# Rows 3 and 4 of a fused attention and squared-ReLU kernel: another order for their loads, copies and transposes

## The chip, the cores and the metric

The kernel runs on one core of a Trainium2 chip. The metric is the device time of one execution in microseconds (us). A core has five engines with an instruction queue each: TensorE (PE in the profile, its weight loads PEld), VectorE (DVE), ScalarE (ACT), GpSimd (POOL) and SyncE (SP), which here only issues DMAs. Every queue is worked off in order: an instruction that waits holds up all that stand behind it on its engine. DMAs are issued from the queues of SP and POOL and carried out by the core's 16 DMA engines.

## The reference

Eight batch rows (`q`, `k`, `v` of 8 heads, 576 positions, 64 dims) go through masked attention. Heads 0 to 3 see a sliding window of 32 positions, heads 4 to 7 see every fourth of the last 128. The result, as 4608 tokens by 512, goes through two matrix products with a squared ReLU between them.

```python
rel = pos[:, None] - pos[None, :]
mask_plain = (rel >= 0) & (rel < 32)
mask_dil = (rel >= 0) & (rel < 128) & (rel % 4 == 0)
scores = where(mask, q @ k.T / sqrt(64), -1e9)
attn = softmax(scores)              # plain mask for heads 0-3, dilated for heads 4-7
x = (attn @ v).transpose(0, 2, 1, 3).reshape(4608, 512)
out = relu(x @ w_in) ** 2 @ w_out   # w_in 512 x 2048, w_out 2048 x 512
```

## The kernel before

The order of all work is written out by hand. Two streams run side by side on TensorE. One is the matrix products, in nine chunks `c` of 512 tokens: first `mm1_gen` (line 263, 16 tiles of 128 features; ScalarE applies the ReLU at line 272 and VectorE squares at line 297), then, for chunks 1 and 2, `mm2_gen` (line 304), and from chunk 3 on `seven_gen` (line 407), which computes the second product with seven instead of eight block products. The other stream is the attention of the rows `b`, eight of them, cut into parts: `z0 z1` (dilated scores, line 613), `s0 s1` (sliding scores, line 599), `d0 d1 e0 e1` (probabilities times `v`, dilated, line 668), `a0 a1 a2` (the same, sliding, line 652), and `y0 y1 x0 x1` (transposes of the result, lines 701 and 683, copied into `xT` by ScalarE at 707 and 689). The products are a Python generator that `pump` advances; `run` pumps to a step number and then issues the part that stands at that step. Chunk `c` carries the attention of row `c+1`; from chunk 2 on it also carries the scores of row `c+2`. So chunk 1 works on row 2, chunk 2 on row 3 and on row 4's scores.

Before the scores of a row can be computed, its `q` and `k` pass through several hands. For the loop's rows this is so:

1. POOL looks (`see`, line 190) at something that has landed, to hold its queue until then, and issues four DMAs: `n` (sliding heads, line 146) and `dd` (dilated heads, line 223, from DRAM to DRAM), `k` and `q` of each, converted to fp16 on the way.
2. `in_token_order` (lines 228 to 236) copies `n` to `o` in token order. For row 2 ScalarE copies 6 of 9 parts and VectorE 3; for every other row VectorE copies all. The step is `ORDER[c]`, so the copy stands in VectorE's queue among that chunk's other work.
3. SP writes `o` to DRAM (`dp`, line 241) and reads both back through the DMA's transpose: `QKTd` from `dd` (line 253), `QKTp` from `dp` (line 249).

The `v` of a row is loaded as fp32 by SP, dilated heads into `sd` (lines 164 and 166, two DMAs) and sliding heads into `sv` (line 156, six DMAs); there is one buffer of each. POOL casts them to fp16: `vd<-sd` in four casts (line 208), `vp<-sv` in three (line 204). `vd` is read by `d0` to `e1`, `vp` by `a0` to `a2`.

At the start of chunk 1 POOL's queue holds: four casts of `sd` (row 2), a look at the last piece of `sv`, a look at row 2's `QKTp`, the four DMAs for row 3, three casts of `sv`. At the start of each later chunk it holds a look at the newest row's `QKTp`, the four DMAs of row `c+2`, four casts of `sd`, three casts of `sv`.

SP's queue from row 3 on, before: `dp`, `QKTd`, `QKTp` of row 3; four stores of chunk 1's results (lines 328, 325, 326); `sd` and `sv` of row 3 (from line 1002, after the chunk); `QKTd`, `dp`, `QKTp` of row 4; `sd` and `sv` of row 4.

PSUM has eight banks. The products and, for rows 2 and 3, the transposed results take turns on four of them (`bank`), the attention takes turns on two pairs (`pair`): a part that wants a pair waits until VectorE has read the part before the last out of it (`normalize`, lines 637 and 638).

Of the kernel before, what the change touches and what calls it, by code (L numbers as in the profile page):

```python
# [17 lines left out]
def kernel(  # L18
# [9 lines left out]
    nc = tc.nc  # L28
# [18 lines left out]
    NB = S // QB  # L47
# [68 lines left out]
    sv = stg.tile([P, NB, HH, D], FP32, name="sv")  # L116
# [26 lines left out]
    def load_whole_sliding_qk(b):  # L143
        n = natp.tile([P, HH, 9, D], FP16, name=f"n{b}", tag="n")
        for i, s in ((1, k), (0, q)):
            nc.gpsimd.dma_start(
                out=n[64 * i : 64 * (i + 1)],
                in_=s[b, 0:HH].rearrange("h (p j) d -> p h j d", j=9),
            )
        return n  # L150

    def load_sliding_v(b, m0=0, m1=NB):
        for m in range(m0, m1):
            lo = QB * m - PADP
            p0 = PADP if m == 0 else 0
            nc.sync.dma_start(
                out=sv[p0:P, m, :, :],
                in_=v[b, 0:HH, lo + p0 : lo + P, :].transpose([1, 0, 2]),
            )

    def load_dilated_v(b, t):
        vv = v[b, HH:H].rearrange("h (i c) d -> i h (c d)", c=DIL)
        if t:
            nc.sync.dma_start(out=sd[:, 1, :, :], in_=vv[QD - PADD : CL])
        else:
            nc.sync.dma_start(out=sd[PADD:P, 0, :, :], in_=vv[0:QD])

    def load_v(b, dilated_first=False):
        if not dilated_first:
            load_sliding_v(b)  # L170
        for t in range(2):
            load_dilated_v(b, t)
        if dilated_first:
            load_sliding_v(b)
# [13 lines left out]
    def see(landed):  # L188

        nc.gpsimd.tensor_copy(look, landed)  # L190
# [22 lines left out]
    def cast_v(b):  # L213
        sliding = [lambda mp=mp: cast_sliding_v(b, mp) for mp in range(NB // 2)]
        dilated = [lambda t=t, a=a: cast_dilated_v(b, t, a) for t in (0, 1) for a in range(2)]
        return dilated + sliding
# [3 lines left out]
    def keep_dilated_qk(b):  # L220
        d = dpool.tile([2, HH * CL, DIL * D], FP16, name=f"dd{b}", tag="dd")
        for i, src in ((1, k), (0, q)):
            nc.gpsimd.dma_start(
                out=d[i], in_=src[b, HH:H].rearrange("h (i c) d -> (h i) (c d)", c=DIL)
            )
        return d

    def in_token_order(b, n):
        o = natp.tile([P, 9, HH, D], FP16, name=f"o{b}", tag="o")
        i = n.rearrange("p h j d -> p j h d")  # L230
        if b == 2:
            nc.scalar.copy(o[:, 0:6], i[:, 0:6])
            nc.vector.tensor_copy(o[:, 6:9], i[:, 6:9])
        else:
            nc.vector.tensor_copy(o, i)  # L235
        return o

    def keep_sliding_qk(b, o):
        d = dpool.tile([2, S, HH * D], FP16, name=f"dp{b}", tag="dp")
        for i in (1, 0):  # L240
            nc.sync.dma_start(
                out=d[i].rearrange("(p j) x -> p (j x)", j=9),
                in_=o[64 * i : 64 * (i + 1)].rearrange("p j h d -> p (j h d)"),
            )
        return d

    def transpose_sliding(b, dp):
        for i in (1, 0):
            nc.sync.dma_start_transpose(out=QKTp[b % 2][:, i, :, PADP:], in_=dp[i])

    def transpose_dilated(b, dd):
        for i in (1, 0):
            nc.sync.dma_start_transpose(out=QKTd[b % 2][:, i, :, KPAD:], in_=dd[i])
# [107 lines left out]
    def sum_w_out_gen():  # L361

        for name, pool, tag, w in (("T1", n1p, "nd", 36), ("T2", n1p, "nd", 36), ("T3", n1p, "ns", 36)):
            u = pool.tile([P, w * D], FP16, name=name, tag=tag, bufs=2 if tag == "nd" else 1)
            T[name] = u[:, 0 : HF * HT].rearrange("p (j t) -> p j t", j=HF)
        for j in range(2):
            f = slice(4 * j, 4 * j + 4)
            b11, b12 = wo[j][:, :, 0:HT], wo[j][:, :, HT:DM]
            b21, b22 = wo[2 + j][:, :, 0:HT], wo[2 + j][:, :, HT:DM]
            for o, a, b in (  # L370
                ("T1", b12, b11),
                ("T3", b22, b12),
                ("T2", b22, T["T1"][:, f, :]),
                ("T4", b21, T["T2"][:, f, :]),
            ):
                nc.vector.tensor_sub(T[o][:, f, :], a, b)
                yield
# [128 lines left out]
    def moe_gen(c):  # L506
        yield from mm1_gen(c)
        yield from mm2_gen(c)

    def moe_seven_gen(c):  # L510
        yield from mm1_gen(c, sums_behind)
        yield from seven_gen(c)
# [220 lines left out]
    def run(*plans, more=()):  # L733


        todo = list(more)
        for plan, parts in plans:
            for w in plan.split():
                step, *names = w.split(":")
                todo += [(int(step), parts[n]) for n in names]  # L740
        at = 0
        for step, part in sorted(todo, key=lambda t: t[0]):
            pump(step - at)
            at = max(at, step)
            part()
        pump(1000)
# [165 lines left out]
    n, dd = load_whole_sliding_qk(2), keep_dilated_qk(2)  # L912
# [5 lines left out]
    def turn(b, n, dd):  # L918
        dp = keep_sliding_qk(b, in_token_order(b, n))
        if b < 4:  # L920
            transpose_dilated(b, dd)
        transpose_sliding(b, dp)
# [15 lines left out]
        more=[(25, lambda: turn(2, n, dd))],  # L938
# [25 lines left out]
        6: (LATER[0], ""),  # L964
    }

    ORDER = {1: 46, 2: 30, 3: 6, 4: 2, 5: 2}
    for c in range(1, NTOKC):
        b = c + 1
        more = []  # L970
        casts = cast_v(b) if b < B else []
        if c == 1:

            for cast in casts[:4]:
                cast()
            casts = casts[4:]
            see(sv[0:1, NB - 1, 0, 0:1])
            more += [(41, leaves) for leaves in kept[2:]]
        if b + 1 < B:
            see(QKTp[b % 2][0:1, 1, 0, PADP : PADP + 1])  # L980
            n, dd = load_whole_sliding_qk(b + 1), keep_dilated_qk(b + 1)

            def turn_and_load(b=b + 1, n=n, dd=dd):
                turn(b, n, dd)
                if b > 3:
                    load_v(b, True)

            if b + 1 > 3:
                more.append(
                    (max(0, ORDER[c] - 4), lambda b=b + 1, dd=dd: transpose_dilated(b, dd))  # L990
                )
            more.append((ORDER[c], turn_and_load))
        for cast in casts:
            cast()
        if c == 1:
            it = sum_w_out_gen()
            more += [(2 + 3 * i, lambda it=it: next(it)) for i in range(8)]
        pending.append(moe_gen(c) if c < SEVEN else moe_seven_gen(c))
        now, ahead = PLANS.get(c, ("", ""))
        run((now, rows_.get(b)), (ahead, rows_.get(b + 1)), more=more)  # L1000
        if c == 1:
            load_v(3, True)


# [28 lines left out]
```

## Time and profile before

| what | us |
|---|---|
| median of three timed runs (lowest, highest) | 308.22 (307.31, 309.99) |
| the profiled execution | 306.96 |
| its span in the profile | 305.0 |
| TensorE busy | 292.7 (96%) |
| VectorE, ScalarE, GpSimd busy | 207.8, 160.8, 68.8 |
| chunk 1 with row 2, on TensorE | 58.7 to 90.4 |
| chunk 2 with row 3, on TensorE | 90.4 to 126.7 |

All times in the profile are counted from the start of the span. 1.96 us of the profiled execution lie outside the span. "L235" is line 235 of the kernel. A name such as `o<-n` is what an instruction writes and reads. In a timeline a bracket `[0.89 <-DVE x_d L638]` says how long the engine was idle before the instruction and what ended the wait. In the chain, which follows the work that ended last back from the end, every line is a start, a length and who held the chain. Issue of a DMA on SP (`SPq`) is the time that SP's queue spent on it, not the transfer.

### The profile page before, as it was taken

The page shows a single profiled execution, that of the slowest core. Times are in us where ns is not written, and L with a number is a line of the kernel's source. Part 1 is how long each engine was busy: PE and PEld are TensorE (multiplying, and loading weights), DVE is VectorE, ACT ScalarE, POOL GpSimd, SP SyncE. Part 2 cuts the span into 40 slices and gives each one's busy share as a digit, 9 for nine tenths or more (in the row PEclk, how much of TensorE's full clock was granted, in tenths as well). Part 3 has the DMA queues.
Part 4 walks back from the last instruction along what each step waited for, and adds up shares of the span by engine and source line. Part 5 has one row for each costly group of instructions (what it writes and reads, how often), then busy time and mean ns, then how long its engine had stood idle before and what let it go on. Part 6 is the DMA issues. An engine that isn't in the chain of part 4 may idle for free.

```text
span 305.0 us, 7775 instructions
## 1 busy us (share of the span) xinstructions
PE 292.7 (96%) x3236; PEld 222.0 (73%) x3236; DVE 207.8 (68%) x379; ACT 160.8 (53%) x284; POOL 68.8 (23%) x113
## 2 busy tenths in 40 slices
PE   3989999999999988999999999999999999999995
PEld 2669855555557745699889988998888886785584
DVE  7675646597633683389787889788868654863674
ACT  2767764878247924766436733674367216405600
POOL 5481008006403243331420542007000000000000
PEclk9999999999999999999999999999999999999999
DMA  6999999599999998997988994894210030021012
GB/s 113 237 197 212 211 212 253 119 173 224 167 282 235 225 204 154 224 270 175 237 227 191 202 210 134 191 207 83 90 49 2 15 126 2 0 71 69 0 37 103
DMA packets 75890, 46.76 MB, mean 153 GB/s; under 512 B 54416, under 2 KB 72080, under 8 KB 75664
## 3 DMA queue, kind: packets, MB, share of 16 engines
q1 hardware_dynamic: 68464, 32.52, 46.4%
q0 software_dynamic: 7248, 13.63, 24.9%
q8 instruction: 25, 0.41, 0.5%
q10 hardware_dynamic: 144, 0.13, 0.1%
q14 instruction: 9, 0.07, 0.1%
HBM read 39.85 MB, written 16.52 MB: 185 GB/s over the span
## 4 chain that ended last, share of the span: by engine, by line
PE 85%; DMA 7%; DVE 3%; POOL 2%; issue 1%; ACT 1%; POOLq 0%; DVEq 0%
PE PS L263 40%; PE PS L407 24%; PE PS L304 11%; DMA wi<-in_moe_w_in_dram 3%; DMA sd<-in_v_dram 2%; PE PS L668 2%; DMA n<-in_q_dram 2%; PE PS L613 2%; PE PS L652 2%; PE PS L599 1%; PE PS L683 1%; PE PS L701 1%; DVE o L235 1%; DVE g L297 1%; ACT AT L580 1%
## 5 line engine op out<-in xcount | busy, mean ns | idle before, releaser
L263 PE MATMUL PS<-xT,wi 128*128 128x288 f16 (+8 forms) x1024 | 135.6, 286 | 0.9 <-DMA wi<-in_moe_w_in_dram 0.9
L272 ACT ACTIVATE rt<-PS 128x512 f16<-128x512 f32 (+2 forms) x160 | 88.9, 556 | 65.6 <-PE PS L263 62.9
L263 PEld LDWEIGHTS <-wi 128*128 128x128 f16 x1024 | 96.9, 114 | 26.7 <-DMA wi<-in_moe_w_in_dram 1.1
L297 DVE TENSOR_TENSOR g<-rt 128x1024 f16<-128x1024 f16 (+1 forms) x64 | 45.6, 712 | 35.9 <-ACT rt L272 35.2
L580 ACT ACTIVATE AT<-PS 128x576 f16<-128x576 f32 x64 | 38.5, 650 | 22.8 <-PE PS L599 14.5
L304 PE MATMUL PS<-wo,g 128*128 128x512 f16 x192 | 49.3, 379 | 0.0
L407 PEld LDWEIGHTS <-S 128*128 128x128 f16 x384 | 37.0, 98 | 4.6
L208 POOL CAST vd<-sd 128x512 f16<-128x512 f32 x32 | 24.0, 782 | 59.0 <-DMA sd<-in_v_dram 39.2
L407 PE MATMUL PS<-T,S 128*128 128x256 f16 x288 | 34.1, 273 | 0.0
L407 PEld LDWEIGHTS <-g 128*128 128x128 f16 x288 | 27.5, 98 | 3.8
L304 PEld LDWEIGHTS <-g 128*128 128x128 f16 x192 | 15.6, 98 | 12.6
L204 POOL CAST vp<-sv 128x512 f16<-128x512 f32 x24 | 18.0, 767 | 25.5 <-DMA sv<-in_v_dram 13.4
L407 PE MATMUL PS<-wo,g 128*128 128x256 f16 x192 | 23.4, 273 | 0.0
L638 DVE TENSOR_TENSOR x_d<-PS,rcp_d 72x512 f16<-72x512 f32 x32 | 22.0, 687 | 1.1
L584 DVE TENSOR_TENSOR AT<-AT,maskd 128x1152 f16<-128x1152 f16 x14 | 11.8, 844 | 12.0 <-ACT AT L580 11.8
L584 DVE TENSOR_TENSOR AT<-AT,maskp 128x1152 f16<-128x1152 f16 x14 | 11.1, 795 | 10.4 <-ACT AT L580 10.4
L638 DVE TENSOR_TENSOR x_p<-PS,rcp_p 96x512 f16<-96x512 f32 (+1 forms) x25 | 16.6, 665 | 0.9
L668 PEld LDWEIGHTS <-AT 128*128 128x128 f16 x256 | 11.9, 100 | 5.2 <-DVE x_d L638 1.8
L707 ACT COPY xT<-PS 128x576 f16<-128x576 f16 x16 | 10.2, 640 | 9.5 <-PE PS L701 8.9
L668 PE MATMUL PS<-vd,AT 128*128 128x65 f16 x256 | 13.8, 197 | 1.0 <-DVE x_d L638 1.0
L689 ACT COPY xT<-PS 128x576 f16<-128x576 f16 x16 | 10.2, 638 | 8.3 <-PE PS L683 7.9
L286 DVE TENSOR_TENSOR g<-rt 128x288 f16<-128x288 f16 x32 | 9.8, 308 | 6.3 <-ACT rt L272 6.2
(89 smaller groups left out, 261.1 us busy)
## 6 DMA issues: line engine op xcount, KB each, us to landing
out_dram<-c SPq DMA_DIRECT2D x23, 256.0 KB, 2.2
sv<-in_v_dram SPq DMA_DIRECT2D x40, 128.0 KB, 6.2
sd<-in_v_dram SPq DMA_DIRECT2D x8, 512.0 KB, 6.6
dp<-o SPq DMA_DIRECT2D x12, 288.0 KB, 4.8
out_dram<-ot SPq DMA_DIRECT2D x11, 256.0 KB, 3.6
sd<-in_v_dram SPq DMA_DIRECT2D x8, 288.0 KB
wo<-in_moe_w_out_dram POOLq DMA_DIRECT2D x4, 512.0 KB, 14.6
n<-in_k_dram POOLq DMA_DIRECT2D x6, 288.0 KB, 6.0
```

The costliest lines, as they stand in the source:

```text
L204: nc.gpsimd.tensor_copy(vp[b % 2][:, m : m + 2, :, 0:D], sv[:, m : m + 2, :, :])
L208: nc.gpsimd.tensor_copy(vd[b % 2][:, t, c : c + 2, :, 0:D], sd[:, t, :, D * c : D * (c + 2)].rearrange("p h (c d) -> p c h d", d=D),)
L263: nc.tensor.matmul(ph[:, a - t0 : b - t0], w_in_of(dmk, ffc), xT[r % 3][:, dmk, a - r * S : b - r * S], start=(dmk == 0 and a == t0), stop ...
L272: nc.scalar.activation(rt, ph[:, 0:w], ACTF.Relu)
L297: nc.vector.tensor_mul(g[:, f2 : f2 + 2, o:TOKC], rt[:, :, o:TOKC], rt[:, :, o:TOKC])
L304: nc.tensor.matmul(po, g[:, ffc, o + t * P : o + (t + 1) * P], w_out_of(ffc), start=(ffc == 0), stop=(ffc == NFF - 1),)
L407: nc.tensor.matmul(po[t], lhs(j)[:, t * P : (t + 1) * P], rhs(j), start=j == 0, stop=j == HF - 1)
L580: nc.scalar.activation(AT[:, u + i, 0:UW], ps[:, :, 0 : UW // 2], ACTF.Exp, scale=scale)
L584: nc.vector.tensor_mul(AT[:, u : u + n, 0:UW], AT[:, u : u + n, 0:UW], mask.unsqueeze(1).to_broadcast([P, n, UW]),)
L638: nc.vector.tensor_tensor(out=x[0:w, 0:n], in0=pv[:, :, :, 0:D], in1=rcp[0:w, 0:n].unsqueeze(3).to_broadcast([w, n, HH, D]), op=ALU.mult,)
L668: nc.tensor.matmul(pav[:, e, h * (D + 2) : h * (D + 2) + D + 1], AT[:, 4 + 2 * a + t, off : off + P], vd[b % 2][:, t, 2 * a + e, h, 0 : D ...
L689: nc.scalar.copy(xT[b % 3][:, 0:2, t0 : t0 + 288], px[:, 0:UW].rearrange("x (c t) -> x c t", c=2),)
```

## The change

It touches rows 3 and 4 only, in five places.

- The copy to token order of row 3 is shared like row 2's (ScalarE 6 parts of 9, VectorE 3); row 4's is ScalarE's alone. Rows 5 to 7 stay with VectorE.
- In chunk 1 only two casts of `sd` stand ahead of row 3's DMAs on POOL, and the look is at the fourth piece of `sv` instead of the sixth. The other two casts of `sd` follow the DMAs.
- The turn of row 4 stands at step 33 of chunk 2 instead of 30.
- Row 3's `sd` is issued on SP right behind its transposes, ahead of the four stores of chunk 1.
- Row 4's `QKTd` transposes are issued at the start of chunk 2, and row 3's `sv` behind them.

For chunks 3 and later the queues hold what they held, in the same order, although the lines are written anew. TensorE's queue is the same from first to last instruction.

SP's queue from row 3 on, after: `dp`, `QKTd`, `QKTp` of row 3; `sd` of row 3; four stores; `QKTd` of row 4; `sv` of row 3; `dp`, `QKTp` of row 4; `sd` and `sv` of row 4.

```diff
@@ in_token_order
-        if b == 2:
-            nc.scalar.copy(o[:, 0:6], i[:, 0:6])
-            nc.vector.tensor_copy(o[:, 6:9], i[:, 6:9])
-        else:
-            nc.vector.tensor_copy(o, i)
+        j = {2: 6, 3: 6, 4: 9}.get(b, 0)
+        if j > 0:
+            nc.scalar.copy(o[:, 0:j], i[:, 0:j])
+        if j < 9:
+            nc.vector.tensor_copy(o[:, j:9], i[:, j:9])
         return o
@@ the loop over chunks
-    ORDER = {1: 46, 2: 30, 3: 6, 4: 2, 5: 2}
+    ORDER = {1: 46, 2: 33, 3: 6, 4: 2, 5: 2}
     for c in range(1, NTOKC):
         b = c + 1
         more = []
         casts = cast_v(b) if b < B else []
         if c == 1:
 
-            for cast in casts[:4]:
+            for cast in casts[:2]:
                 cast()
-            casts = casts[4:]
-            see(sv[0:1, NB - 1, 0, 0:1])
+            casts = casts[2:]
+            see(sv[0:1, 3, 0, 0:1])
             more += [(41, leaves) for leaves in kept[2:]]
         if b + 1 < B:
             see(QKTp[b % 2][0:1, 1, 0, PADP : PADP + 1])
@@
             def turn_and_load(b=b + 1, n=n, dd=dd):
                 turn(b, n, dd)
+                load_dilated_v(b, 0)
+                load_dilated_v(b, 1)
                 if b > 3:
-                    load_v(b, True)
+                    load_sliding_v(b)
 
             if b + 1 > 3:
-                more.append(
-                    (max(0, ORDER[c] - 4), lambda b=b + 1, dd=dd: transpose_dilated(b, dd))
-                )
+                transpose_dilated(b + 1, dd)
+            if b == 3:
+                load_sliding_v(3)
             more.append((ORDER[c], turn_and_load))
@@
         run((now, rows_.get(b)), (ahead, rows_.get(b + 1)), more=more)
-        if c == 1:
-            load_v(3, True)
```

## The prediction

> **What bounds the kernel now.** I read the busy times first, then the same by chunk, then the chain of waits through chunks 1 and 2, then the timelines of TensorE, ScalarE, POOL and SP there. The page's busy times, and TensorE's share in the windows of chunk 1 (58.7 to 90.4), chunk 2 and the next three stretches (columns: window, its length, busy PE, PEld, DVE, ACT, POOL, clock, DMA share, GB/s):
>
> ```profile
> PE 292.7 (96%) x3236; PEld 222.0 (73%) x3236; DVE 207.8 (68%) x379; ACT 160.8 (53%) x284; POOL 68.8 (23%) x113
> ...
> 58.70:90.40 31.70, 30.81 (x269) 17.23 (x268) 20.03 (x34) 17.91 (x33) 8.21 (x13) 1.00 1.05 213
> 90.40:126.70 36.30, 34.57 (x388) 21.96 (x387) 18.99 (x30) 21.91 (x39) 13.09 (x21) 1.00 1.03 212
> 126.70:158.00 31.30, 31.30 (x384) 27.29 (x383) 24.72 (x43) 18.58 (x32) 8.52 (x14) 1.00 0.98 225
> ```
>
> TensorE bounds everything. What it idles is 31.70 - 30.81 = 0.89 us in chunk 1 and 36.30 - 34.57 = 1.73 us in chunk 2, and nothing from 126.7 to 275. TensorE's work is untouched by the change, so all that can be won is in these 2.62 us. The timeline of TensorE has them as three waits:
>
> ```profile
> 84.08 0.30 PE L701 MATMUL PS<-ident,x_d 72*128 72x72 f16 x4 [0.89 <-DVE x_d L638]
> ...
> 110.56 0.43 PE L668 MATMUL PS<-vd,AT 128*128 128x65 f16 x8 [0.95 <-DVE x_d L638]
> ...
> 118.04 0.31 PE L613 MATMUL PS<-QKTd 64*128 64x72 f16 x8 [0.78 <-DVE x_p L638]
> ```
>
> Each ends with VectorE's normalization. The chain shows what made the first two late: the copy to token order, L235, stands ahead of it. In chunk 1 it waits for row 3's `n`, in chunk 2 VectorE is simply behind.
>
> ```profile
> 75.40 0.63 POOL n L146
> 76.02 5.73 DMA n<-in_q_dram
> ...
> 81.83 1.35 DVE o L235
> 83.19 0.12 DVE rcp_d L637
> ...
> 83.33 0.70 DVE x_d L638
> ...
> 105.35 1.10 DVE g L297
> 106.45 1.26 DVE o L235
> 107.71 0.94 DVE AT L584
> 108.65 1.01 DVE g L297
> ```
>
> **Row 3's copy (chunk 1).** POOL casts `sd` from 69.99 to 73.85, looks at the last `sv` piece until 74.72 and issues `n` at 75.40. With two casts it is through at about 72 and waits for the fourth piece; the pieces land some 0.5 us apart, so the look ends 1 us earlier and `n` is asked at 74.4. The DMA share in slices of 1 us is 0.08 at 75 and 0.49 at 76, so there is room, and `n` lands at 80.75 instead of 81.75. VectorE's share then takes 0.54 us (row 2's, L233) instead of 1.35 and is over at 81.3, not 83.2. Then 0.19 + 0.69 us of reciprocal and x_d: ready at 82.3. TensorE wants it at 84.08 - 0.89 = 83.19. Even if `n` lands no sooner, the shorter copy alone saves 0.81 of 0.89. Gain: 0.89, bounds 0.81 and 0.89; what is late next on that path has 0.9 us of slack.
>
> ScalarE's share is 1.47 us (row 2's, L232), 80.75 to 82.2. Behind it stand the `xT` copy (now at 79.98) and the store's copy (80.85); they go to 82.2 and 82.9, over at 83.5. The PSUM bank of the latter is taken again by the fourth result tile at 86.5: 2 to 3 us of slack, cost nothing. The two moved casts come after the look and four DMA issues (75.40 to 77.64, so 76.6 to 78); `e0`, which reads the first of them (done at 77.3), starts at 78.41: cost nothing, with 1.1 us of cover. The whole of row 3's `o` is ready at 82.2 instead of 83.2, and the SP chain behind it (`dp` 83.21, `QKTd` 85.26, `QKTp` 89.01 to 91.79), the look (92.49) and row 4's DMAs (93.06 to 95.3) all come 0.9 us sooner, as TensorE does.
>
> **Row 4's copy (chunk 2).** 1.34 us leave VectorE. ScalarE pays: the rows 576 elements in 0.639 us and 1536 in 1.474 give 0.87 ns for one more, so 2304 take 2.14 us; in proportion to the latter alone, 2.21. ScalarE idles 4.53 us before its copy at 111.88 (from 107.36), the copy at step 33 falls into that hole, and `n` has long landed (asked 93.69, 7.3 us). Cost nothing; without the hole, 2.2 us. On VectorE the mask of `s1` then waits for ScalarE's exponential (over at 106.87), and 0.76 + 0.69 + 0.2 + 0.69 us later x_d is there, 109.3, where TensorE wants it at 109.61. Gain 0.95. The lower bound comes from the same rows as they ran beside POOL's casts, 0.94 + 1.01 instead of 0.76 + 0.69: 109.8, gain 0.75.
>
> VectorE's product L297 takes 0.69 us at 94.75 with POOL silent and 1.10 at 105.35 while POOL casts `sd` (105.10 to 108.04). [...]
>
> The third wait (0.78) stays: the second score tile wants the PSUM pair that `a1`'s x_p frees, and `a1` itself ran just ahead of it on TensorE.
>
> **Row 3's `v`.** `sd` is issued at 91 instead of 94.66, ahead of four stores, which nothing waits for soon. POOL waits 9.76 us for it now and casts at 105.10, against a first use at 107.2; earlier is no loss. The risk is `sv`. Before, the first cast of it ran at 107.99 on POOL, and SP's timeline had
>
> ```profile
> 95.76 11.26 SPq L156 DMA_DIRECT2D sv<-in_v_dram  x6
> 107.14 3.52 SPq L253 DMA_TRANSPOSE QKTd<-dd  x2
> ```
>
> Now `sv` stands behind the two transposes, and these wait for row 4's `dd`. Its second half is asked at 94.80 and lands 9.2 us later (chunk 3: 10.1). Asked 0.9 us sooner it lands at 103.1 to 104.0; the last transpose is issued by 105.5, the first two `sv` pieces by 106.5. Recorded pieces took 3.6 to 7.5 us from issue to landing in this chunk, 5.0 to 6.0 in row 2's. With the queue empty by then I take the lowest: 109.6, cast (0.65) over at 110.3. `a0`, now at 113.50, will want it at 113.50 - 0.89 - 0.95 = 111.66. Cost 0; at 6.0 us it is 1.0. Behind `sv` on SP stands row 4's `dp`, now at 110.75, then at 109 to 110, so `QKTp` is not later against `s0` at 124.4.
>
> Against the early `sd` stands a row: in chunk 3, with `sd` 0.7 us ahead of it, the first `n` took 7.7 us to land, in chunk 2 with stores ahead 4.7. That is the 10.1 above. [...] I go by the row.
>
> **Sum.** 306.96 - 0.89 - 0.95 = 305.1 for an execution like the profiled one (305.0 of span and 1.96 outside). The median of the runs shown is 1.26 above it, 308.22; the same 1.84 off gives **306.4**. That is 0.6%, under the 1% or so that a measurement of this kernel can tell from no change.
>
> **Rivals.**
>
> *`sv` becomes the wait (20%).* Row 3's own second `sv` piece, in a crowded queue, needed 107.56 - 96.36 = 11.2 us. Asked at 106 it would land at 117, be cast at 117.8, and `a0` would stand 6.2 us: 308.22 - 1.84 + 6.2 = 312.6. At 6 us of landing it is 307.4. It decides from the first `vp` cast ending after 113.5 (then the gain is gone); after 116.6 it is over 1% slower. For it: a DMA share near 1 from 88 to 114. Against: all that crowded the queue before, POOL's four DMAs, has landed when `sv` is issued.
>
> *The gain goes elsewhere (12%).* VectorE's work is there, but POOL's casts or the next wait on a PSUM pair take its place, as with the 0.78. Then 307.5 to 308.2.
>
> *It does only half of what it says (6%).* `n` is asked 1 us sooner at most, since the look still waits for `sv`, and if ScalarE gets `n` late in chunk 2 its 2.2 us hold the copies at 111.88 and 112.37. Price up to 1.5: 307.9.
>
> *More than the sum (7%).* With VectorE ahead, the third wait shrinks too: 2.62 off, 305.6, and a bit below with lucky runs.
>
> Forecast as worked out: 55%, 305.4 to 307.4 with the spread of the runs.
>
> **Range and chances.** The lower end takes the whole 2.62 and the runs' own spread of 0.9: 304.7. The upper takes the `sv` rival halfway, 308.22 - 1.84 + 3.1 = 309.5. Faster by over 1% (under 305.1): 0.12. Slower by over 1% (over 311.3): 0.08, all from the crowded `sv`. Within: 0.80.
>
> **What would show it.** Right: in chunk 1 no wait of TensorE on x_d near 83, DVE's copy of `o` 0.54 us; in chunk 2 ScalarE's copy of 2.1 to 2.2 us between the last ReLU and the store's copy, no wait at `e0`; POOL's casts of `sd` before 101; `vp` cast by 110.3; the 0.78 still there. Wrong: TensorE waiting at L652 for a `vp` cast, or SP's `sv` issues stretched as the 11.26 us were.

## The result, and the profile after

| | before | after |
|---|---|---|
| median, 11 runs each (lowest, highest) | 309.88 (307.17, 312.07) | 305.99 (303.99, 310.53) |
| ratio, 95% interval | | 0.989 [0.985, 0.993] |
| profiled execution | 306.96 | 304.84 |
| its span | 305.0 | 303.1 |
| chunk 1, from its first product to chunk 2's | 31.73 | 30.67 |
| chunk 2 | 36.51 | 35.38 |
| chunk 3 to the end | 178.03 | 178.05 |

Ratios, here and below, leave out runs over 1.5% above the fastest of the same kernel, while a median is of all runs. The forecast was 306.4 for the median and 305.1 for an execution like the profiled one. The profiled execution took 2.12 us less where 1.84 were forecast. In two later comparisons the same kernel stood at 0.9937 and 1.0011 times the kernel before. So 1.1% is the best of three occasions, and the experiments below deal with that too. By the means of all runs the three are closer together: 0.992, 0.993 and 0.997.

Busy times on the page of the kernel after, and TensorE's share by chunk (window, length, then busy PE, PEld, DVE, ACT, POOL, clock, DMA share, GB/s; chunks 1, 2 and 3):

```profile
PE 292.3 (96%) x3236; PEld 222.1 (73%) x3236; DVE 204.0 (67%) x378; ACT 163.9 (54%) x286; POOL 69.3 (23%) x113
```

```profile
58.97:89.64 30.67, 30.67 (x270) 17.19 (x269) 19.10 (x34) 19.17 (x34) 8.04 (x13) 1.00 1.05 220
89.64:125.02 35.38, 34.60 (x389) 22.13 (x388) 17.10 (x29) 24.13 (x40) 11.08 (x20) 1.00 0.94 207
125.02:156.70 31.68, 31.68 (x388) 27.82 (x387) 26.25 (x43) 18.33 (x32) 10.12 (x15) 1.00 1.04 221
```

Length and busy PE are equal in chunks 1 and 3. Chunk 2 keeps 0.78 us of idle time. About 3.8 us of work have gone from VectorE, and 3.1 came to ScalarE, which has the room. The timeline of TensorE around the places of the second and third wait:

```profile
108.65 0.42 PE L668 MATMUL PS<-vd,AT 128*128 128x65 f16 x8
...
111.58 0.42 PE L652 MATMUL PS<-vp,AT 128*128 128x65 f16 x8
...
116.12 0.31 PE L613 MATMUL PS<-QKTd 64*128 64x72 f16 x8 [0.78 <-DVE x_p L638]
```

`e0` (L668) and `a0` (L652) start without a wait. Only the third wait is left. In the chain of waits, too, nothing but TensorE holds chunks 1 and 2, except where VectorE's normalization causes that 0.78:

```profile
115.38 0.70 DVE x_p L638
```

The timelines of VectorE, then ScalarE, show the shared copies:

```profile
80.90 0.55 DVE L235 COPY o<-n 128x768 f16<-128x768 f16 x1 [0.83 <-DMA n<-in_q_dram]
```

```profile
80.89 1.47 ACT L233 COPY o<-n 128x1536 f16<-128x1536 f16 x1 [3.65 <-DMA n<-in_q_dram]
...
106.42 2.13 ACT L233 COPY o<-n 128x2304 f16<-128x2304 f16 x1
109.97 0.58 ACT L314 COPY ot<-PS 128x512 f32<-128x512 f32 x1 [1.41 <-PE PS L304]
```

The 2.13 us of row 4's copy fill a hole: ScalarE still idles 1.41 us behind it. The timelines of POOL and of SP show row 3's `v`:

```profile
96.66 1.17 POOL L208 CAST vd<-sd 128x512 f16<-128x512 f32 x2 [1.86 <-DMA sd<-in_v_dram]
98.84 1.17 POOL L208 CAST vd<-sd 128x512 f16<-128x512 f32 x2 [1.01 <-DMA sd<-in_v_dram]
110.67 0.61 POOL L204 CAST vp<-sv 128x512 f16<-128x512 f32 x1 [10.66 <-DMA sv<-in_v_dram]
```

```profile
91.12 0.50 SPq L166 DMA_DIRECT2D sd<-in_v_dram  x1
...
104.46 2.78 SPq L253 DMA_TRANSPOSE QKTd<-dd  x2
107.36 3.51 SPq L156 DMA_DIRECT2D sv<-in_v_dram  x6
```

The first `vp` cast ends at 111.28, and `a0` starts at 111.58. The forecast had 110.3 and 111.66. The cover of `a0`, the time by which what it reads is early, is 0.3 us. That narrow place is where the experiments turned out to matter most.

### The profile page after: what moved, and what is told of

It is laid out like the page before. It is cut to its first block, busy times and chain, and to the rows that moved or that the text cites. A ratio compares the mean times of both kernels' runs of the same rounds, so it can differ in the third digit from the quotient of the medians.

```text
span 303.1 us, 7778 instructions
## 1 busy us (share of the span) xinstructions
PE 292.3 (96%) x3236; PEld 222.1 (73%) x3236; DVE 204.0 (67%) x378; ACT 163.9 (54%) x286; POOL 69.3 (23%) x113
## 4 chain that ended last, share of the span: by engine, by line
PE 91%; DMA 5%; POOL 2%; issue 1%; DVE 0%; POOLq 0%
PE PS L263 41%; PE PS L407 25%; PE PS L304 14%; DMA wi<-in_moe_w_in_dram 3%; DMA sd<-in_v_dram 3%; PE PS L668 2%; PE PS L652 2%; PE PS L613 2%; PE PS L599 2%; PE PS L683 1%; PE PS L701 1%; PE PS L534 0%; POOL ns L131 0%; POOL nd L138 0%; POOL vp L204 0%
## 5 line engine op out<-in xcount | busy, mean ns | idle before, releaser
L263 PE MATMUL PS<-xT,wi 128*128 128x288 f16 (+8 forms) x1024 | 135.6, 286 | 1.0 <-DMA wi<-in_moe_w_in_dram 0.9
L263 PEld LDWEIGHTS <-wi 128*128 128x128 f16 x1024 | 96.9, 114 | 26.8 <-DMA wi<-in_moe_w_in_dram 1.2
L297 DVE TENSOR_TENSOR g<-rt 128x1024 f16<-128x1024 f16 (+1 forms) x64 | 44.4, 694 | 35.5 <-ACT rt L272 34.8
L304 PE MATMUL PS<-wo,g 128*128 128x512 f16 x192 | 49.3, 379 | 0.0
L208 POOL CAST vd<-sd 128x512 f16<-128x512 f32 x32 | 25.2, 820 | 49.6 <-DMA sd<-in_v_dram 49.6
L304 PEld LDWEIGHTS <-g 128*128 128x128 f16 x192 | 15.6, 98 | 12.6
L204 POOL CAST vp<-sv 128x512 f16<-128x512 f32 x24 | 16.3, 695 | 36.7 <-DMA sv<-in_v_dram 29.8
L668 PEld LDWEIGHTS <-AT 128*128 128x128 f16 x256 | 12.0, 100 | 4.0 <-DVE x_p L638 0.5
L668 PE MATMUL PS<-vd,AT 128*128 128x65 f16 x256 | 13.8, 197 | 0.0
```

The costliest lines, as they stand in the source:

```text
L204: nc.gpsimd.tensor_copy(vp[b % 2][:, m : m + 2, :, 0:D], sv[:, m : m + 2, :, :])
L208: nc.gpsimd.tensor_copy(vd[b % 2][:, t, c : c + 2, :, 0:D], sd[:, t, :, D * c : D * (c + 2)].rearrange("p h (c d) -> p c h d", d=D),)
L263: nc.tensor.matmul(ph[:, a - t0 : b - t0], w_in_of(dmk, ffc), xT[r % 3][:, dmk, a - r * S : b - r * S], start=(dmk == 0 and a == t0), stop ...
L297: nc.vector.tensor_mul(g[:, f2 : f2 + 2, o:TOKC], rt[:, :, o:TOKC], rt[:, :, o:TOKC])
L304: nc.tensor.matmul(po, g[:, ffc, o + t * P : o + (t + 1) * P], w_out_of(ffc), start=(ffc == 0), stop=(ffc == NFF - 1),)
L668: nc.tensor.matmul(pav[:, e, h * (D + 2) : h * (D + 2) + D + 1], AT[:, 4 + 2 * a + t, off : off + P], vd[b % 2][:, t, 2 * a + e, h, 0 : D ...
```

## The experiments

The theory: the two waits on x_d are all that the change wins; the copies of rows 3 and 4 and the earlier `n` win it, while the new order on SP wins nothing and only puts `a0` at risk. The rivals: the order on SP is what helps; or `sv` is about to become the wait.

Lengths in this table are of TensorE: where chunk 1 starts, how long chunks 1 and 2 and the rest are, and the idle time with a named releaser in each (us, one profiled execution each).

| kernel | chunk 1 starts | chunk 1 (idle) | chunk 2 (idle) | rest | ratio |
|---|---|---|---|---|---|
| before | 58.70 | 31.73 (0.89) | 36.51 (1.73) | 178.03 | 1 |
| before_again | 59.15 | 31.73 (0.90) | 36.15 (1.36) | 178.05 | |
| after | 58.97 | 30.67 (0) | 35.38 (0.78) | 178.05 | 0.989 [0.985, 0.993] |
| after_again | 62.13 | 30.82 (0) | 35.48 (0.78) | 178.02 | 0.9937 [0.9895, 0.9979] |
| after_third | 58.80 | 30.66 (0) | 36.49 (1.72) | 179.91 | 1.0011 [0.9971, 1.0051] |
| e1_copies | 59.54 | 31.72 (0.88) | 35.53 (0.78) | 178.02 | 0.9958 [0.9925, 0.9991] |
| e2_asked | 59.28 | 31.64 (0.80) | 35.83 (1.04) | 178.03 | 0.9941 [0.9912, 0.997] |
| e3_queue | 60.77 | 32.17 (1.34) | 36.23 (1.43) | 178.02 | 1.0044 [1.0012, 1.0076] |
| e6_no_queue | 60.04 | 30.66 (0) | 35.54 (0.78) | 178.04 | 0.9892 [0.9839, 0.9945] |
| e5_a1 | 60.59 | 31.06 (0.22) | 35.79 (1.10) | 178.77 | 0.9916 [0.9876, 0.9955] |
| e7_no_queue_a1 | 60.43 | 30.66 (0) | 34.67 (0) | 178.19 | 0.9886 [0.9832, 0.994] |
| e9_sv_first_a1 | 61.04 | 30.66 (0) | 34.53 (0) | 179.96 | 0.9889 [0.9818, 0.9961] |
| e8_late_sv | 60.29 | 30.66 (0) | 45.15 (8.39) | 178.03 | |
| e4_late_sv | 58.85 | 31.28 (0.45) | 35.39 (0.78) | 182.26 | |

The runs fall into three comparisons, each on a chip of its own with its own runs of the kernel before: e1, e2, e3 and before_again; then after_again, e6, e5 and e4; then e7, e9, e8 and after_third. The second table follows row 3's `n` (its `q` half), counted from the start of chunk 1: when it was asked for, how long it was in flight, and when it landed.

| kernel | asked | in flight | landed | TensorE's wait |
|---|---|---|---|---|
| before, before_again (copy 1.35) | 17.32, 17.27 | 5.73, 5.79 | 23.05, 23.06 | 0.89, 0.90 |
| e3_queue (copy 1.35) | 17.13 | 6.37 | 23.50 | 1.34 |
| e2_asked (copy 1.35) | 17.04 | 5.93 | 22.97 | 0.80 |
| e1_copies (copy 0.56) | 17.19 | 6.66 | 23.85 | 0.88 |
| e5_a1 (copy 0.55) | 16.53 | 6.66 | 23.19 | 0.22 |
| e4_late_sv (copy 0.56) | 17.04 | 6.37 | 23.41 | 0.45 |
| after, after_again, after_third, e6 to e9 (copy 0.55) | 16.00 to 16.62 | 5.18 to 5.41 | 21.41 to 21.91 | 0 |

### Each part alone

**e1_copies**: only the shared copies of rows 3 and 4, and row 4's step.

```diff
+        j = {2: 6, 3: 6, 4: 9}.get(b, 0)
+        if j > 0:
+            nc.scalar.copy(o[:, 0:j], i[:, 0:j])
+        if j < 9:
+            nc.vector.tensor_copy(o[:, j:9], i[:, j:9])
...
-    ORDER = {1: 46, 2: 30, 3: 6, 4: 2, 5: 2}
+    ORDER = {1: 46, 2: 33, 3: 6, 4: 2, 5: 2}
```

> The kernel before with the copies alone changed: row 3's shared 6 to 3 between ScalarE and VectorE, row 4's on ScalarE at step 33; loads and queues as before. Theory A (the copies on VectorE made both waits): row 3's n lands at 81.75 as before, VectorE is through at 82.3, x_d is there at 83.2, so the 0.89 us wait in chunk 1 shrinks to 0.1 or less; in chunk 2 POOL's casts of sd still run at 105 to 108 beside VectorE, so 0.1 to 0.3 us of the 0.95 stays. Span shorter by 1.5 to 1.8 us, ratio 0.994 to 0.995. Theory B (the order on SP and POOL gives more than the two waits, because the runs of before lose time to transfers that the profile did not show): well under half of the 1.1% that was measured, 0.996 or more.

Measured: 306.65, ratio 0.9958 [0.9925, 0.9991]. The wait at `e0` is gone, but chunk 1's stayed. VectorE's timeline, then TensorE's:

```profile
83.47 0.56 DVE L235 COPY o<-n 128x768 f16<-128x768 f16 x1 [2.83 <-DMA n<-in_q_dram]
```

```profile
84.91 0.30 PE L701 MATMUL PS<-ident,x_d 72*128 72x72 f16 x4 [0.88 <-DVE x_d L638]
```

VectorE idles 2.83 us for `n`, copies for 0.56, and TensorE still waits 0.88. The short copy did what it should; `n` came 0.8 us later than in the kernel before (23.85 against 23.05). The second table shows it for all kernels: landing less TensorE's wait is 22.16 or 22.17 with the long copy (four executions) and 22.96 or 22.97 with the short one (three). So sharing row 3's copy moves the latest harmless landing by 0.81 us, exactly the forecast's figure, but the landing itself scatters by more (21.41 to 23.85 in the table).

**e2_asked**: only row 3's earlier request.

```diff
-            for cast in casts[:4]:
+            for cast in casts[:2]:
                 cast()
-            casts = casts[4:]
-            see(sv[0:1, NB - 1, 0, 0:1])
+            casts = casts[2:]
+            see(sv[0:1, 3, 0, 0:1])
```

> The kernel before with row 3's q and k asked for sooner alone (two casts ahead of it and the look at the fourth piece of sv); the copies stay whole on VectorE. Theory A: n lands 0.9 us sooner, at 80.8; VectorE copies until 82.2, x_d at 83.1, so the wait in chunk 1 is almost gone by this part alone too (0.1 or less left); chunk 2 keeps 0.75 to 0.95 us at e0 since row 4's copy is still VectorE's. Span shorter by 0.8 to 1.0 us, ratio 0.997. Theory B: 0.994 or less.

Measured: 306.77, ratio 0.9941 [0.9912, 0.997]. TensorE's timeline:

```profile
84.57 0.30 PE L701 MATMUL PS<-ident,x_d 72*128 72x72 f16 x4 [0.80 <-DVE x_d L638]
...
110.36 0.43 PE L668 MATMUL PS<-vd,AT 128*128 128x65 f16 x8 [0.27 <-DVE x_d L638]
```

In this execution POOL's look at the fourth piece of `sv` ended only 15.75 us into chunk 1 (14.90 in the kernel after). So `n` was asked 0.28 us sooner than before and landed 0.08 sooner, and TensorE's wait is 0.09 shorter. By this profile the run says little about the edit, and it doesn't explain a ratio below the expected 0.997; the intervals of e1 and e2 overlap, so the runs don't rank the two parts either. The edit is judged by the seven executions of the table's last row, where `n` is asked 0.7 to 1.3 us sooner, flies some 0.4 us shorter and lands before 22.16. In those even the long copy would have been in time. In e5 and e4 it landed later than that, and the short copy then left 0.22 and 0.45 where the long one would have left 1.03 and 1.25.

**e3_queue**: only the order on SP.

```diff
                 turn(b, n, dd)
+                load_dilated_v(b, 0)
+                load_dilated_v(b, 1)
                 if b > 3:
-                    load_v(b, True)
+                    load_sliding_v(b)
             if b + 1 > 3:
-                more.append(
-                    (max(0, ORDER[c] - 4), lambda b=b + 1, dd=dd: transpose_dilated(b, dd))
-                )
+                transpose_dilated(b + 1, dd)
+            if b == 3:
+                load_sliding_v(3)
...
-        if c == 1:
-            load_v(3, True)
```

> The kernel before with SP's order alone changed: row 3's sd ahead of the stores, row 4's QKTd transposes next, row 3's sv behind them; copies and asking as before. Theory A: the wait in chunk 1 stays 0.9; in chunk 2 POOL's casts of sd run at 97 to 101 instead of 105 to 108, so VectorE's two products and the mask take 0.7 to 0.8 instead of 0.95 to 1.1 us each and most of the 0.95 us wait goes although the copy is still there (0.1 to 0.3 left). sv lands at about 112, and the first vp cast ends at or before the 112.7 at which a0 comes, 0 to 0.5 us of wait. Span shorter by 0.3 to 0.9 us, ratio 0.997 to 0.999. Theory B: this is where the rest of the gain is, ratio 0.994 or less.

Measured: 309.00, ratio 1.0044 [1.0012, 1.0076], slower. TensorE's timeline, then SP's:

```profile
86.59 0.30 PE L701 MATMUL PS<-ident,x_d 72*128 72x72 f16 x4 [1.34 <-DVE x_d L638]
...
115.72 0.41 PE L652 MATMUL PS<-vp,AT 128*128 128x65 f16 x8 [0.65 <-POOL vp L204]
```

```profile
107.77 4.02 SPq L253 DMA_TRANSPOSE QKTd<-dd  x2
111.91 3.58 SPq L156 DMA_DIRECT2D sv<-in_v_dram  x6
```

The wait at `e0` went here too: `sd` is cast from 100.46, and VectorE's products L297 around the copy, now without casts beside them, take 0.69 and 0.68 us (1.10 and 1.09 before). In its place TensorE waits at `a0` for the `vp` cast. The order gives with one hand and takes with the other. Chunks 1 and 2 together are only 0.16 us longer than in the kernel before; this execution also starts chunk 1 2.07 us later, where the edit touches nothing, so the profile doesn't explain all of the 0.44%.

**before_again**: the kernel before, once more, for the spread of its waits.

> The kernel before, unchanged, for a second profile. Theory A: the same three waits of TensorE, 0.9, 0.95 and 0.8 us within 0.3, and no other between 58 and 290. Theory B: a longer span than 305.0, with the waits in chunks 1 and 2 longer by 1 us or more where n, dd or sv land later.

Measured: 307.07. The waits are 0.90, 0.58 and 0.78. The second is not a constant: it was 0.95 in the first profile.

### Without the new order, and the sum again

**e6_no_queue**: copies and earlier request, with the order on SP as before (the diff of e3 taken back).

> Copies and asking as in the changed kernel, SP's order as before. Theory A: chunk 1 without a wait (30.7 us); in chunk 2 sd is cast at 105 to 108 beside VectorE, which costs 0 to 0.2 us at e0, and sv is on time, so 35.4 to 35.7 us. Together as fast as the changed kernel within 0.1%. Theory B (SP's order carries part of the gain): slower than the changed kernel by 0.3% or more.

Measured: 305.51 in six runs, ratio 0.9892 [0.9839, 0.9945]. TensorE's timeline has one wait in both chunks, and POOL's shows where `sv` now stands:

```profile
117.33 0.31 PE L613 MATMUL PS<-QKTd 64*128 64x72 f16 x8 [0.78 <-DVE x_p L638]
```

```profile
105.84 3.58 POOL L208 CAST vd<-sd 128x512 f16<-128x512 f32 x4 [9.70 <-PE PS L599]
109.37 1.72 POOL L204 CAST vp<-sv 128x512 f16<-128x512 f32 x3
```

All that the change wins is there without the order on SP. All three `vp` casts are over at 111.09, before `a0`'s time of 112.6 (start of chunk 2, 90.70, plus the 21.94 us after which `a0` stood in the kernel after).

**after_again**: the kernel after, unchanged, on the same chip as e6.

> The changed kernel once more, timed on the same chip as the next ones. Theory A (two waits of TensorE removed, 1.8 to 2.2 us between the starts of chunks 1 and 3, and nothing else): a ratio of 0.993 to 0.994, the 1.1% of the first measurement being partly scatter of what lies ahead of chunk 1. Theory B (more than the two waits): again 0.990 or less. Profile: chunk 1 30.7 us and chunk 2 35.3 to 35.8 from the start of one chunk's first product to the next one's, 178.0 behind them.

Measured: 308.08 over all 12 runs, ratio 0.9937 [0.9895, 0.9979]. Chunks 1 and 2 are as in the first profile (30.82, 35.48). The execution is longer because chunk 1 starts at 62.13, 3.2 us later. TensorE had waited ahead of it, in chunk 0, for an x_d that was late behind row 2's `n`:

```profile
57.99 0.43 PE L668 MATMUL PS<-vd,AT 128*128 128x65 f16 x8 [1.85 <-DVE x_d L638]
```

Between 60 us and the start of chunk 1 the granted clock was 0.50 (1.00 in the first profile, without a wait there), and four products L304 took 1.90 us at 60.43, where four take 1.02 in chunk 1. The change touches nothing in that stretch. Over the 14 profiles that start lies between 58.70 and 62.13, a wider spread than the whole gain. That is why the lengths of the chunks are compared, not the times alone.

**after_third**: the same on the third chip.

> The changed kernel beside the three others on one chip. Theory A: ratio 0.992 to 0.995; chunk 1 30.7 to 30.9, chunk 2 35.3 to 35.8 us, no wait for a vp cast. Theory B (sv is too close): a wait of 0.2 us or more for a vp cast at L652.

Measured: 308.93 in 12 runs, ratio 1.0011 [0.9971, 1.0051]: no gain. TensorE's timeline of the profiled execution (307.63):

```profile
112.51 0.41 PE L652 MATMUL PS<-vp,AT 128*128 128x65 f16 x8 [0.94 <-POOL vp L204]
...
117.04 0.30 PE L613 MATMUL PS<-QKTd 64*128 64x72 f16 x8 [0.78 <-DVE x_p L638]
...
134.42 0.43 PE L668 MATMUL PS<-vd,AT 128*128 128x65 f16 x8 [1.69 <-DVE x_d L638]
```

Chunk 1 is 1.07 us shorter than before, as always. The other gain is gone, with 0.94 at `a0`, and a wait of 1.69 is new in chunk 3. There VectorE's copy of row 5 waits for `n`, which landed at 131.50 (the profile puts this wait down to an `sv` load, but the copy reads only `n`). It was asked late. SP issues row 4's `dp` behind the six of `sv`, at 112.25 (110.96 in the first profile); `QKTp`, which reads it, followed 4.9 us later (3.5), at 117.18 (114.49), and POOL's look at `QKTp`, ahead of the request for `n`, ended at 121.2 (118.6). This one profile explains a run without gain; that all 12 runs have these waits isn't shown.

### The place of the next limits

**e5_a1**: the kernel after with chunk 2's `a1` two steps sooner, against the third wait.

```diff
-            SOON.format(18, 22, 26, 30) + " " + EARLY.format(34, 36, 38, 40, 41, 43, 45, 49, 51, 54, 59),
+            SOON.format(18, 22, 26, 30) + " " + EARLY.format(34, 36, 38, 40, 41, 43, 45, 47, 51, 54, 59),
```

> The changed kernel with part a1 of chunk 2 at step 47 instead of 49, two steps ahead of the score part z0 that wants its PSUM pair. Theory A: the third wait of TensorE (0.78 us at L613) is gone, a1 itself comes 0.9 us sooner, at 113.8, when the second vp cast has been over for 0.7 us: chunk 2 34.5 to 34.8 us, 0.25% under the changed kernel. Theory B (sv is the next limit at once): TensorE waits for a vp cast at L652 and half of the 0.78 or more is given back.

Measured: 306.75, ratio 0.9916 [0.9876, 0.9955]. The third wait is gone, and others stand in TensorE's timeline:

```profile
114.86 0.41 PE L652 MATMUL PS<-vp,AT 128*128 128x65 f16 x8 [1.10 <-POOL vp L204]
...
134.80 0.43 PE L668 MATMUL PS<-vd,AT 128*128 128x65 f16 x8 [0.57 <-DVE x_d L638]
```

**e7_no_queue_a1**: e6 with the same step for `a1`.

> Copies and asking as in the changed kernel, SP's order as in the kernel before, and part a1 of chunk 2 at step 47. Theory A (with SP's old order sv is cast by 111.3, 2 us and more ahead of a1, so that the third wait of TensorE can go without a new one): chunk 1 30.7, chunk 2 34.7 to 34.9 us, no wait of TensorE from chunk 1 on; ratio 0.989 to 0.992 and 0.25% under the changed kernel. Theory B (something else takes the 0.78 us, as in the run with the new SP order): chunk 2 35.4 or more.

Measured: 305.95, ratio 0.9886 [0.9832, 0.994], on the chip where the kernel after stood at 1.0011 beside it. The windows of chunks 1 and 2:

```profile
60.43:91.09 30.66, 30.66 (x270) 17.17 (x268) 19.06 (x34) 19.18 (x34) 7.79 (x13) 1.00 1.06 220
91.09:125.76 34.67, 34.67 (x389) 21.91 (x388) 16.96 (x29) 24.03 (x40) 11.71 (x19) 1.00 0.97 201
```

TensorE never idles there. In this comparison it is the version that beats both kernels: copies and request of the change, SP's order of the kernel before, `a1` at step 47.

**e9_sv_first_a1**: e5 with `sv` ahead of row 4's `QKTd` on SP; `sd` stays early.

```diff
-            if b + 1 > 3:
-                transpose_dilated(b + 1, dd)
             if b == 3:
                 load_sliding_v(3)
+            if b + 1 > 3:
+                transpose_dilated(b + 1, dd)
```

> The changed kernel with a1 at step 47 and, on SP, row 3's sv ahead of row 4's QKTd transposes (sd still ahead of the stores). Theory A (the sv behind the transposes was the only thing that held a1): sv is cast well before 111, chunk 2 34.5 to 34.8 us, no wait of TensorE. Theory B: a wait at L652 or L613 of 0.5 us or more stays.

Measured: 306.93, ratio 0.9889 [0.9818, 0.9961]. Chunk 2 is clean, at 34.53, and in the profiled execution (308.0) chunk 3 gives all of it back. Three of the six runs took 305.0 to 305.9, so how many have that wait isn't shown. TensorE's timeline, then VectorE's:

```profile
134.76 0.43 PE L668 MATMUL PS<-vd,AT 128*128 128x65 f16 x8 [1.75 <-DVE x_d L638]
```

```profile
131.92 1.35 DVE L235 COPY o<-n 128x2304 f16<-128x2304 f16 x1 [2.42 <-DMA n<-in_q_dram]
```

The limit in chunk 3 can be read from three runs: row 5's `n` landed 5.61 us (e9), 5.55 (after_third) and 4.43 (e5) after the start of chunk 3, and TensorE waited 1.75, 1.69 and 0.57. Landing less wait is 3.86 each time. Before the change `n` landed 0.68 after that start (127.62 against 126.94): 3.2 us of cover. In the kernel after it is 3.48 (128.50 against 125.02), 0.4 us of cover, with TensorE 1.92 sooner and `n` 0.88 later. In e7 it is 3.85 (129.61 against 125.76): no wait, but no cover either.

**e8_late_sv**: the rival made true. Row 3's `sv` is issued behind row 4's `dp` and `QKTp`, and its casts stand behind it.

```diff
                 turn(b, n, dd)
+                if b == 4:
+                    load_sliding_v(3)
+                    for cast in late:
+                        cast()
...
-            if b == 3:
-                load_sliding_v(3)
             more.append((ORDER[c], turn_and_load))
+        late = []
+        if c == 2:
+            casts, late = casts[:4], casts[4:]
```

> The changed kernel with row 3's sv behind row 4's dp and QKTp on SP, and its three casts behind that load also in the program. Theory A (TensorE waits for sv one for one): sv is issued from about 116, the first cast is over at about 120.5, and TensorE waits some 8.5 us at L652 for a0; span 311 to 313. Theory B (order in a queue matters little): span under 306.

Measured: 315.9, span 314.1. SP's, POOL's and TensorE's timelines:

```profile
116.38 3.24 SPq L156 DMA_DIRECT2D sv<-in_v_dram  x6
```

```profile
120.00 0.61 POOL L204 CAST vp<-sv 128x512 f16<-128x512 f32 x1 [19.40 <-DMA sv<-in_v_dram]
```

```profile
120.67 0.60 PE L652 MATMUL PS<-vp,AT 128*128 128x65 f16 x8 [7.61 <-POOL vp L204]
```

From SP's first issue to the end of the first cast it is 4.2 us (3.9 in the kernel after), so `a0` follows the issue one for one. Chunk 2 grew by 9.77 us, more than the 7.61; the rest, 2.16, goes with a granted clock of 0.52 over the 4.33 us behind the wait (4.33 x 0.48 = 2.08), told at the end.

**e4_late_sv**: a first form of e8 in which the casts were left ahead of the load. Row 3's sliding heads are therefore computed with row 2's `v`, and `a0` waits for nothing.

```diff
                 turn(b, n, dd)
+                if b == 4:
+                    load_sliding_v(3)
...
-            if b == 3:
-                load_sliding_v(3)
```

> The changed kernel with row 3's sv moved further back on SP, behind row 4's dp and QKTp. Theory A (the order on SP's queue decides when sv comes, and TensorE waits for it one for one): sv is issued from 114 on, the first cast is over at 117 to 118, and TensorE waits 5 to 6.5 us at L652 for a0; the span is that much longer than 303.1. Theory B (a queue's order matters little since the transfers share the DMA engines anyway): under 2 us.

Measured: 309.55, and none of the expected wait at `a0`, so it says nothing of that rival. Here row 4's `v` is what comes late: its `sd` is issued at 119.47 instead of 117.40, behind the six of `sv`, and cast from 130.93 instead of 122.39. TensorE's timeline in chunk 3:

```profile
131.59 0.41 PE L668 MATMUL PS<-vd,AT 128*128 128x65 f16 x8 [2.42 <-POOL vd L208]
```

## Why the prediction was right, and where it was not

*The sum.* Right in mechanism. Both waits on x_d are gone: 0.89 and 0.95. The chunks shortened by 1.06 and 1.13, so each wait was worth 0.17 to 0.18 more than its bracket. Against that, this execution started chunk 1 0.27 later. 1.06 + 1.13 - 0.27 - 0.02 is the 1.90 of the span; another 0.22 came outside the span. That the median came so close (305.99 for 306.4) is luck: the two medians lie 3.89 us apart, twice the 1.84, and the 308.22 from which the forecast counted is the median of three runs, where eleven have 309.88. The forecast gain of 0.6% lies outside the first interval (0.7 to 1.5%) and inside the second comparison's.

*Row 3's copy.* Right: `n` landed at 80.82 (forecast 80.75) and the short copy took 0.55 (0.54). The landing is in part luck: from the start of chunk 1 `n` was asked 0.88 us sooner instead of 1, flew 0.32 shorter, which the forecast didn't have, and that start came 0.27 later. "Even if `n` lands no sooner, the shorter copy alone saves 0.81" is right as a shift of the limit (22.16 to 22.97) but no floor under the gain: in e1 `n` landed 0.8 later and the gain was 0.01. The lower bound of 0.81 left out the scatter of a landing, 5.18 to 6.66 us in flight.

*Row 4's copy.* Right: 2.13 us on ScalarE (2.14 by the row), in the hole, at no cost. The wait it removes was put at 0.95; the kernel before has 0.95 in one profile and 0.58 in another, and e2, which leaves this copy as it was, has 0.27. So the gain is 0.3 to 0.95, from execution to execution.

*POOL's casts.* The rows of the kernel after agree with the 0.69 and 1.10 us that the prediction read before: with the casts gone to 96.66 to 100.0, the product L297 beside them (97.45) takes 0.92, and those from 102 on take 0.68 or 0.69. But e1 and e6 lost the wait at `e0` with the casts still beside, so that move was not needed.

*The third wait.* Right, 0.78 in every kernel that doesn't move `a1`.

*Row 3's `v`: the step that failed in size.* "Asked 0.9 us sooner it lands at 103.1 to 104.0" was too early. `dd` was asked at 94.27, 0.5 us sooner, and landed at 105.94, 11.7 us later. A second miss hid part of this: the `sv` pieces flew 2.6 to 3.0 us in the kernel after, where the forecast took 3.6, the lowest of its rows. At 3.6 the first cast would have ended some 1 us later, behind the time of `a0`, so the cover that is left is luck. The flights of `dd` separate cleanly. With `sd` behind the stores, six executions (before, before_again, e1, e2, e6, e7) have 8.7 to 9.2 us. With `sd` ahead of them, all eight have more: 11.4 to 13.2 in after, after_again, after_third, e3, e5 and e9, and 10.5 and 10.8 in e4 and e8, where row 3's `sv` is issued later still. The prediction's row (the first `n` 7.7 us in flight with `sd` ahead of it, 4.7 with stores ahead) pointed this way, and the runs do so more strongly than the row. They don't show by which mechanism. The cover of `a0` became 0.3 us instead of 1.4, "cost 0" held in two of three profiled executions of the kernel after, and the third paid 0.94. The condition of the rival was right (e8), and its price of 0.65 to 1.10 us (after_third, e3, e5) is at the low end of what it gave.

*What no step had.* Row 5's copy in chunk 3. The prediction checked `QKTp` against `s0`, but not the chain behind it: look, request, `n`, VectorE's copy, x_d. It also had row 4's `dp` at 109 to 110, sooner than before; it went at 110.96, and in after_third at 112.25. TensorE comes there 1.9 us sooner while the DMAs do not.

*Open.* The ratio's move from 0.989 to 1.0011 between comparisons (0.992 to 0.997 by the means of all runs). Two waits explain one profile of the last, and the start of chunk 1 scatters by 3.4 us besides; how often those waits occur in the runs without a profile isn't known.

## What to carry to other kernels

Test the parts of a bundled change alone and without each other: here two parts carried the gain, and the third, a reordered DMA queue, added a risk and, beside those two, nothing else. For each wait work out the latest harmless arrival (arrival less wait, from several profiles) and compare it with the scatter of arrivals: a cover thinner than the scatter is a gain on some runs only. When the bounding engine comes sooner, look at the next chain of DMAs that it meets, since that has lost as much cover.

## What the runs showed of the hardware

- A wait costs TensorE more than its bracket: chunk 1 is 30.66 or 30.67 long in six of the seven executions without a wait (the seventh, after_again, is 30.82 long; it enters it at a granted clock of 0.50 and has 0.99 over its length), and its length less the wait is 30.83 or 30.84 in all seven that had one, 0.17 us more.
- After the 7.61 us of idle time in e8 the granted clock was 0.52 over the next 4.33 us, and four products L304 took 1.90 us instead of about 1.03. The clock also fell with shorter waits: to 0.50 from 60 to 62 us in after_again, behind a wait of 1.85 us (four products L304 in 1.90 us instead of 1.02), from 133 to 136 in e4, behind 2.42 (twelve products L263 in 2.45 us, and in 1.47 from 136.62 on), and from 20 to 23 in e9, around a wait of 1.80 ahead of chunk 1 (eight products L263 in 2.11 us, and the next eight in 1.19). It stayed at 1.00 behind the 1.75 us in chunk 3 of e9 and the 1.69 in after_third (twelve products L263 in 1.47 us ahead of the wait and behind it, in both). What decides whether it falls isn't shown. The waits that the change removes, 0.89 and 0.95 us, are below all of these, and the clock was 1.00 behind them.
- What was asked sooner mostly flew shorter too: `n` asked up to 16.62 us into chunk 1 flew 5.2 to 5.4 us in seven of eight executions (6.66 in e5); asked at 17.04 or later it flew 5.7 to 6.7 in all six. Why isn't shown.
